# One small tile for the row sums and reciprocals of two attention tiles

## The chip, the cores and the metric

One core of a Trainium2 chip runs the whole program. The metric is the device time in microseconds (us) of one execution; of the kernel before there are three runs, 902.25, 906.55 and 906.75 us, with a median of 906.55 us.

## The reference

Three blocks follow each other, all in float32. The sizes are batch B = 4, heads H = 8, sequence S = 576, head size 64, model width 512.

```python
scores = scale * (q_rot @ k_rot.T)              # 576 x 576 for each batch and head
scores = scores - scores.max(-1)
attn = exp(scores); attn = attn / (attn.sum(-1) + 1e-9)
x = attn @ v                                    # to (4, 576, 512)
x = sigmoid(xr @ w_r) * (relu(xk @ w_k)**2 @ w_v)   # xk, xr: mixes of x and x shifted by a token
u = x + (relu(x.T @ w_tok1) @ w_tok2).T
out = u + relu(u @ w_ch1) @ w_ch2
```

## The kernel before

**Tiles.** A group g is one batch and one pair of heads, so there are 16 groups. A group has ND = 9 tiles of 128 query rows by 576 keys: r = 0 to 7 are four couples (even r for one head, odd r for the other, the same 128 rows), and r = 8 holds the last 64 rows of both heads. Tiles are numbered j = 9 g + r, 144 in all. The first 36 (batch 0, `j < FIRST`) and the other 108 are handled in two ways.

**One tile.** `emit_S` (L452) makes the scores on TensorE in a PSUM tile "S", for both tiles of a couple together. `emit_max` (L470) takes the negated row maximum on VectorE. `emit_exp` (L478, L486) takes the exponential on ScalarE and has the row sum written out by an accumulator read, a second instruction of one column. For r in ASIDE = (0, 2, 4, 6, 7) the exponentials go to an SBUF tile called "es"; for r = 1, 3, 5, 8 they stay in place in PSUM, and the row sum goes to a spare PSUM column beside them. `emit_rc` (L498, L500) makes a denominator and its reciprocal on VectorE, two operations of 128 x 1 for each tile. `emit_hi` (L82) scales the exponentials by the reciprocal into float16 on ScalarE; `emit_lo` (L511) computes the float16 remainder on VectorE and so frees the PSUM of a tile in place; `emit_tr` (L594, L596) transposes both by DMA from SyncE's queue. `emit_pv` (L609) multiplies by v on TensorE: 28 products for the rows of r = 0 to 3, and 28 for those of r = 4 to 8, which come three steps into the next group.

**Batch 0.** There the exponentials stay unscaled: they are transposed on TensorE, multiplied by v (`emit_U`, L546), and a product of the reciprocals with the identity (L550) spreads these for the scaling of the result (`emit_Us`). It already waits for both tiles of a couple.

**What else runs there.** While the tiles of batches 1 to 3 go through (about 113 to 405 us of the profile), `prep` rotates, splits and loads q, k and v of later groups (VectorE, ScalarE, GpSimd, SyncE), and `kvr_gen` runs the relu-squared products of batches already done on TensorE, with conversions on ScalarE and GpSimd ("kp", "t", "q", "k", "vp"). Five of its eight chunks run beside attention; the others wait until attention is over (HELD).

**What sets the order.** `a_step(j)` emits the work of a step; a planner then orders the instructions of each engine by emission position, moved ahead by the constants of PRI (hi 400, S 400, den 50), and by a timeline that it simulates. The engines run their queues in that order. Score tiles have three PSUM buffers, so the scores of a couple need the exponential of the couple before (even tile) and the remainder of an odd tile before that.

In step j of batches 1 to 3 the order of emission is: exponential of j, maximum of j + 1, other work, denominator, reciprocal and hi of j, lo and transpose of j - 1, other work, scores of the next couple, `prep`.

Of the kernel before, what the change touches and what calls it, by code (L numbers as in the profile page):

```python
# [7 lines left out]
F32 = mybir.dt.float32  # L8
# [5 lines left out]
AF = mybir.ActivationFunctionType  # L14
# [5 lines left out]
HS = 288  # L20
DM, DFF, DTOK, DCH = 512, 1024, 256, 1536
KD, KF, KC = DM // 128, DFF // 128, DCH // 128
PSCALE = 2.0 ** 14
# [4 lines left out]
ND = 9  # L28
# [17 lines left out]
ASIDE = (0, 2, 4, 6, 7)  # L46
# [25 lines left out]
def body(tc, kin, qin, vw, tabs, ident, mu, w_k, w_v, w_r, w_t1, w_t2, w_c1, w_c2, out):  # L72
    nc = tc.nc
    PS = bass.MemoryType.PSUM
    act, dve, pool, pe, sp = nc.scalar, nc.vector, nc.gpsimd, nc.tensor, nc.sync

    def copy(e, o, i, scale=None):
        if e == "A":
            if scale is None:
                act.activation(out=o, in_=i, func=AF.Copy)  # L80
            else:
                act.activation(out=o, in_=i, func=AF.Copy, scale=scale)  # L82
        elif e == "P":
            pool.tensor_scalar(out=o, in0=i, scalar1=1.0 if scale is None else scale, scalar2=0.0,
                               op0=ALU.mult, op1=ALU.add)
        elif scale is None:
            dve.tensor_copy(o, i)
        else:
            dve.tensor_scalar(out=o, in0=i, scalar1=scale, scalar2=None, op0=ALU.mult)
# [12 lines left out]
    def prio(name):  # L102
        def wrap(f):
            def g(*a):
                with ahead(PRI.get(name, 0)):
                    return f(*a)
            return g
        return wrap
# [5 lines left out]
    with ctx:  # L114
# [60 lines left out]
        def order(o, p, how=mybir.DependencyClass.NoSync):  # L175
            tc.add_manual_dep(o.ins, p.ins.name, mybir.DependencyInfo(how, mybir.DependencyReason.DATA), reason="order")
# [101 lines left out]
        def right(name, bufs):  # L278
            return at.enter_context(tc.tile_pool(name=name, bufs=bufs, side="right"))
# [8 lines left out]
        p16_p = right("p16", BUFS["p16"])  # L288
        pt_p = right("pt", BUFS["pt"])
        sm_p = right("sm", BUFS["sm"])  # L290
# [10 lines left out]
        FIRST, NTT = NP * ND, NG * ND  # L301
# [106 lines left out]
            sp.dma_start(t[0:64, 5:9], t[64:128, 0:4])  # L408
            sp.dma_start(t[64:128, 5:9], t[0:64, 1:5])

        S_t, sum_t, p16_t, e_t, T_t, U_t, rc_t, free = {}, {}, {}, {}, {}, {}, {}, {}
        pt_t, xT = {}, {}

        def place(r):

            return (4, 0) if r == ND - 1 else (r // 2, r % 2)
# [15 lines left out]
        def emit_S(js):  # L432
            with ahead(PRI["S0" if js[0] < FIRST else "S"]):
                S_products(js)
# [37 lines left out]
        @prio("exp")  # L472
        def emit_exp(j):

            if j < FIRST:
                s = sm_p.tile([128, 1], F32, tag="vm", name="es")
                e = e_t[j] = p16_p.tile([128, 2, HS], F32, tag="p16", name="e")
                act.activation(out=e, in_=S_t.pop(j)[:, :, 0:HS], func=AF.Exp, bias=sum_t[j], accum_out=s)  # L478
                sum_t[j] = s
                return  # L480
            s = S_t[j][:, 0, HS:HS + 1]
            i = e_t[j] = S_t.pop(j)[:, :, 0:HS]
            if j % ND in ASIDE:
                s = sm_p.tile([128, 1], F32, tag="vm", name="es")
                e_t[j] = kz_p.tile([128, 2, HS], F32, tag=f"kz{j % 2}{j // 2 % 2}", name="es")
            o = act.activation(out=e_t[j], in_=i, func=AF.Exp, bias=sum_t[j], accum_out=s)  # L486
            if j % ND in ASIDE:
                free[j] = o
            sum_t[j] = s

        @prio("den")
        def emit_rc(j):
            n = j % ND % 2 if j < FIRST else 0
            if n == 0:
                rc_t[0] = sm_p.tile([128, 2], F32, tag="rc", name="rc")
            r = rc_t[0][:, n:n + 1]
            d = sm_p.tile([128, 1], F32, tag="den", name="den")
            dve.tensor_scalar(out=d, in0=sum_t[j], scalar1=1e-9, scalar2=1.0 if j < FIRST else 1.0 / PSCALE,  # L498
                              op0=ALU.add, op1=ALU.mult)
            dve.reciprocal(r, d)  # L500
            sum_t[j] = rc_t[0] if j < FIRST else r

        @prio("hi")
        def emit_hi(j):
            t = p16_t[j] = p16_p.tile([128, 2, 2, HS], F16, tag="p16", name="p16")
            copy("A", t[:, 0], e_t[j], sum_t[j])

        @prio("lo")
        def emit_lo(j):
            t = p16_t[j]  # L510
            o = last["lo"] = dve.scalar_tensor_tensor(out=t[:, 1], in0=e_t.pop(j), scalar=sum_t[j], in1=t[:, 0],  # L511
                                                      op0=ALU.mult, op1=ALU.subtract)
            if j % ND not in ASIDE:
                free[j] = o

        @prio("tr")
        def emit_T(j):

            t = S_p.tile([128, 2, 512], F32, tag="S", name="T")
            e = e_t.pop(j).rearrange("p a b -> p (a b)")  # L520
            t = T_t[j] = t.rearrange("p a b -> p (a b)")[:, 0:640].rearrange("p (c q) -> p c q", c=5)
            for c in range(5):
                o = min(128 * c, S - 128)
                pe.transpose(t[:, c], e[:, o:o + 128], idn)
# [8 lines left out]
        @prio("pv")  # L533
        def emit_U(j):

            g, r = divmod(j, ND)
            m = place(r)[0]
            p = U_t[g, m] = pv_p.tile([128, 512], F32, tag="pv", name="U")
            ts, w = [T_t.pop(i) for i in ([j] if r == ND - 1 else [j - 1, j])], 64 if r == ND - 1 else 128
            q = None  # L540
            for c in range(6):
                for x in range(2):
                    l = slice(64 * x, 64 * x + 64)
                    d = l if r == ND - 1 else slice(0, 128)
                    if c < 5:
                        o = pe.matmul(p[l, 0:w], lhsT=v_t[g][:, c, l], rhs=ts[x % len(ts)][:, c, d], start=(c == 0),  # L546
                                      stop=(c == 4))
                    else:
                        a = sum_t[j][:, 0:1] if r == ND - 1 else sum_t[j - 1 + x][:, x:x + 1]
                        o = pe.matmul(p[l, 128:128 + w], lhsT=a.broadcast_to([128, 64]), rhs=idn[:, d], start=True,  # L550
                                      stop=True)
                    if q is not None:
                        order(o, q)
                    q = o
# [32 lines left out]
        @prio("tr")  # L587
        def emit_tr(j):
            g, r = divmod(j, ND)
            m, x = place(r)  # L590
            t = p16_t[j].rearrange("p a b c -> p (a b c)")
            if r == ND - 1:
                for y in range(2):
                    sp.dma_start_transpose(out=pt(g, y, 1)[:, :, 256:320], in_=t[64 * y:64 * y + 64])  # L594
            else:
                sp.dma_start_transpose(out=pt(g, x, m // 2)[:, :, 128 * (m % 2):128 * (m % 2) + 128], in_=t)  # L596
# [69 lines left out]

        after = {}

        def a_step(j, kv):

            g, k = divmod(j, ND)

            def other():
                with ahead(PRI["kv"]):
                    kv(KVN)

            if j < NTT:
                emit_exp(j)
            late = group(j + 1) if j + 1 == FIRST else []
            if j + 1 < NTT and not late:  # L680
                emit_max(j + 1)
            other()
            if j < FIRST:
                emit_T(j)
                emit_rc(j)
            elif j < NTT:
                emit_rc(j)
                emit_hi(j)
            for gg in (g, g - 1):
                r = j - gg * ND  # L690
                if NP <= gg < NG and r in PV_AT:
                    after.setdefault(j + 1, []).append(emit_pv(gg, PV_AT[r]))
            if 0 <= j - 1 < FIRST:
                emit_ev(j - 1)
            elif FIRST <= j - 1 < NTT:
                emit_lo(j - 1)
                emit_tr(j - 1)
            other()
            if late:
                emit_S(late)  # L700
                emit_max(j + 1)
            elif j + 2 != FIRST and group(j + 2):
                emit_S(group(j + 2))
            def whole(i):
                return 0 <= i < FIRST and (i % ND % 2 or i % ND == ND - 1)

            if whole(j - 1):
                emit_U(j - 1)
                emit_Us(j - 1)
            for f in after.pop(j, []):  # L710
                f()
            other()
            prep(g, k + ND)
            prep(g + 1, k)
            prep(g + 2, k - ND)
# [487 lines left out]
        n = 0  # L1203
# [7 lines left out]
        n = 0  # L1211
# [79 lines left out]
```

## Time and profile before

| | |
|---|---|
| profiled execution | 908.21 us, its span 906.0 us |
| median of three runs | 906.55 us (902.25 to 906.75) |
| busy over the span | PE 843.6, PE weight loads 726.6, DVE 636.2, ACT 513.9, POOL 476.2 us |
| granted clock, mean over the span | 0.977 |

PE is TensorE, DVE VectorE, ACT ScalarE, POOL GpSimd, SP SyncE. Busy time is the time in which at least one instruction of the engine runs. A bracket such as [1.60 <-DVE rc L500] behind a line of a timeline says how long the engine stood idle before it and what ended that. Attention of batch 0 runs from about 14 to 110 us, of the other batches from 113 to 405 us; the rest is dense layers.

### The profile page before, as it was taken

How to read it: one execution, taken by the hardware profiler on the slowest of the kernel's cores; microseconds unless marked ns; L12 is line 12 of the kernel's file. 1: busy time of each engine (PE TensorE's matmuls, PEld its weight loads, DVE VectorE, ACT ScalarE, POOL GpSimd, SP SyncE). 2: the span in 40 equal slices, each digit the busy share in tenths (PEclk: the TensorE clock that was granted, in tenths of full speed). 3: DMA queues.
4: the chain of work that ended last, by engine and by line, in shares of the span. 5: the costliest groups of instructions: out<-in, count | busy, mean ns of one | idle time of the engine just before them, and what ended most of it. 6: DMA issues, size and time to landing. Idle time of an engine off the chain costs nothing.

```text
span 906.0 us, 18800 instructions
## 1 busy us (share of the span) xinstructions
PE 843.6 (93%) x7004; PEld 726.6 (80%) x7004; DVE 636.2 (70%) x1468; ACT 513.9 (57%) x1155; POOL 476.2 (53%) x506
## 2 busy tenths in 40 slices
PE   8999859898977889999999999999999999999998
PEld 5888747777766778889999989988878888888876
DVE  4889788887888889750794699956798354546332
ACT  2889668776777778774565566454456322323221
POOL 6799979889788676355444654411132222222221
PEclk7999969999999999999999999999999999999999
DMA  8687389998998988889522231201230001001000
GB/s 243 228 270 229 101 181 202 194 217 182 200 203 163 202 147 164 154 160 343 180 90 96 96 116 60 76 2 36 76 95 24 1 5 49 27 27 53 2 27 27
DMA packets 168651, 112.07 MB, mean 124 GB/s; under 512 B 132720, under 2 KB 148208, under 8 KB 168048
## 3 DMA queue, kind: packets, MB, share of 16 engines
q1 hardware_dynamic: 168560, 110.87, 49.2%
q8 instruction: 55, 0.90, 0.4%
q14 instruction: 36, 0.29, 0.1%
HBM read 60.90 MB, written 14.16 MB: 83 GB/s over the span
## 4 chain that ended last, share of the span: by engine, by line
PE 48%; DVE 16%; POOL 6%; ACT 6%; issue 5%; DMA 4%; SPq 1%; DVEq 0%; ACTq 0%; POOLq 0%
PE co L737 5%; PE c1p L737 5%; PE c1p L738 5%; PE c1p L739 5%; PE co L738 5%; PE co L739 5%; DVE p L511 4%; PE pv L609 2%; DVE nm L470 2%; PE vp L737 2%; PE vp L738 2%; PE vp L739 2%; DMA pt<-p 2%; PE kp L737 1%; PE S L452 1%
## 5 line engine op out<-in xcount | busy, mean ns | idle before, releaser
L111 POOL TENSOR_TENSOR hs<-ht,hs 128x288 f16<-128x288 f32 x96 | 73.3, 764 | 229.6 <-DVE ht L1170 115.5
L1166 ACT ACTIVATE hs<-c1p,top 128x288 f16<-128x288 f32 x96 | 47.7, 497 | 161.7 <-PE c1p L739 161.7
L470 DVE TENSOR_REDUCE nm<-S 128x1 f32<-128x576 f32 x144 | 104.5, 749 | 24.8 <-PE S L452 24.0
L738 PE MATMUL c1p<-uhl,parts 128*128 128x288 f16 x384 | 109.8, 286 | 0.0
L739 PE MATMUL c1p<-uhl,parts 128*128 128x288 f16 x384 | 109.7, 286 | 0.0
L737 PE MATMUL c1p<-uhl,parts 128*128 128x288 f16 x384 | 109.5, 286 | 0.0
L738 PE MATMUL co<-hs,parts 128*128 128x288 f16 x384 | 108.7, 286 | 0.0
L739 PE MATMUL co<-hs,parts 128*128 128x288 f16 x384 | 108.6, 286 | 0.0
L737 PE MATMUL co<-hs,parts 128*128 128x288 f16 x384 | 105.1, 286 | 0.3 <-ACT hs L1166 0.3
L452 PE MATMUL S<-kq 64*128 64x288 f32 (+1 forms) x696 | 79.4, 326 | 17.4 <-ACT es L486 5.0
L737 PEld LDWEIGHTS <-parts 128*128 128x128 f16 x768 | 75.1, 98 | 19.3 <-issue 0.5
L738 PEld LDWEIGHTS <-parts 128*128 128x128 f16 x768 | 75.1, 98 | 18.9
L739 PEld LDWEIGHTS <-parts 128*128 128x128 f16 x768 | 75.2, 98 | 18.6
L737 PE MATMUL kp<-xs,parts 128*128 128x288 f32 x256 | 80.1, 316 | 9.0 <-ACT t L805 8.0
L452 PEld LDWEIGHTS S<-kq 64*128 64x128 f32 (+1 forms) x696 | 62.4, 200 | 32.3 <-ACT es L486 9.9
L1170 DVE TENSOR_SCALAR ht<-c1p,top 128x288 f32<-128x288 f32 x60 | 30.9, 516 | 77.6 <-ACT hs L1166 76.5
L111 POOL TENSOR_TENSOR q<-t 128x288 f32<-128x288 f32 x64 | 52.4, 823 | 58.8 <-ACT t L805 55.0
L737 PE MATMUL vp<-k,parts 128*128 128x288 f32 x256 | 76.5, 304 | 4.9 <-ACT vt L830 3.9
L738 PE MATMUL vp<-k,parts 128*128 128x288 f32 x256 | 76.2, 300 | 0.9 <-DVE k L111 0.9
L511 DVE SCALAR_TENSOR_TENSOR p<-es,rc,p 128x576 f16<-128x576 f32 x60 | 68.2, 1141 | 12.4 <-ACT p L82 12.4
L738 PE MATMUL kp<-xs,parts 128*128 128x288 f32 x256 | 76.3, 298 | 0.0
L739 PE MATMUL kp<-xs,parts 128*128 128x288 f32 x256 | 75.7, 296 | 0.0
(158 smaller groups left out, 2467.2 us busy)
## 6 DMA issues: line engine op xcount, KB each, us to landing
rq<-in_qin_dram SPq DMA_DIRECT2D x30, 320.0 KB, 4.1
rk<-in_kin_dram SPq DMA_DIRECT2D x30, 288.0 KB, 3.7
words<-in_w_c_dram SPq DMA_DIRECT2D x12, 512.0 KB, 3.9
words<-in_w_c_dram SPq DMA_DIRECT2D x16, 384.0 KB, 3.2
vr<-in_vw_dram SPq DMA_DIRECT2D x16, 320.0 KB, 3.5
xd<-xT SPq DMA_DIRECT2D x16, 288.5 KB, 2.6
xT<-xd SPq DMA_DIRECT2D x4, 1154.0 KB, 5.4
vd<-vt SPq DMA_DIRECT2D x32, 144.0 KB, 2.2
```

The costliest lines, as they stand in the source:

```text
L111: return (pool if e == "P" else dve).tensor_tensor(o, a, b, op=op)
L452: o = pe.matmul(S_t[j][:, h, 0:HS], lhsT=a[l, 128 * m:128 * m + 128], rhs=b[l, h * HS:(h + 1) * HS], start=(n == 0), stop=(n == 2))
L470: last["max"] = dve.tensor_reduce(out=nm, in_=S_t[j][:, :, 0:HS], op=ALU.max, axis=AX.XY, negate=True)
L511: o = last["lo"] = dve.scalar_tensor_tensor(out=t[:, 1], in0=e_t.pop(j), scalar=sum_t[j], in1=t[:, 0], op0=ALU.mult, op1=ALU.subtract)
L609: pe.matmul(p[l, 0:n], lhsT=v[:, a, l], rhs=ts[x][:, c, :], start=(i == 0), stop=(i == len(prods) - 1))
L737: pe.matmul(p, lhsT=wh, rhs=t[:, 0], start=first, stop=False)
L738: pe.matmul(p, lhsT=wh, rhs=t[:, 1], start=False, stop=False)
L739: pe.matmul(p, lhsT=wl, rhs=t[:, 0], start=False, stop=last)
L1166: last["hs"] = act.activation(out=h[:, 0], in_=p[:, 0:HS], func=AF.Relu, scale=g)
L1170: dve.tensor_scalar(out=f, in0=p[:, 0:HS], scalar1=g, scalar2=0.0, op0=ALU.mult, op1=ALU.max)
```

## The change

A tile "es" of 128 x 6 is allotted at the first tile of each couple, and at r = 8. Columns 0 and 1 take the two row sums, 2 and 3 the denominators, 4 and 5 the reciprocals. The accumulator of an exponential in place writes to it too. `emit_rc` runs once for a couple, with two columns (one for r = 8), and in the step of the second tile. In batches 1 to 3 hi of both tiles, then lo and transpose of both, the second tile first, follow in that same step; so hi of an even tile is emitted one step later than before, and lo and transpose of an odd tile and of r = 8 one step earlier.

```diff
 def emit_exp(j):
+    n = j % ND % 2
+    if n == 0:
+        both[0] = sm_p.tile([128, 6], F32, tag="es", name="es")
+    t = both[0]
+    s = t[:, n:n + 1]
+    i = S_t.pop(j)[:, :, 0:HS]
...
-    s = S_t[j][:, 0, HS:HS + 1]
-    i = e_t[j] = S_t.pop(j)[:, :, 0:HS]
-    if j % ND in ASIDE:
-        s = sm_p.tile([128, 1], F32, tag="vm", name="es")
...
     o = act.activation(out=e_t[j], in_=i, func=AF.Exp, bias=sum_t[j], accum_out=s)
...
-    sum_t[j] = s
+    sum_t[j] = t[:, 4 + n:5 + n]

 def emit_rc(j):
-    n = j % ND % 2 if j < FIRST else 0
-    if n == 0:
-        rc_t[0] = sm_p.tile([128, 2], F32, tag="rc", name="rc")
-    r = rc_t[0][:, n:n + 1]
-    d = sm_p.tile([128, 1], F32, tag="den", name="den")
-    dve.tensor_scalar(out=d, in0=sum_t[j], ...)
-    dve.reciprocal(r, d)
+    t, w = both[0], 1 if j % ND == ND - 1 else 2
+    d = t[:, 2:2 + w]
+    dve.tensor_scalar(out=d, in0=t[:, 0:w], ...)
+    dve.reciprocal(t[:, 4:4 + w], d)

+def whole(j):
+    return j % ND % 2 or j % ND == ND - 1
+def tiles(j):
+    return [j] if j % ND == ND - 1 else [j, j - 1]

 def a_step(j, kv):
     if j < FIRST:
         emit_T(j)
+        if whole(j):
+            emit_rc(j)
+    elif j < NTT and whole(j):
         emit_rc(j)
-    elif j < NTT:
-        emit_rc(j)
-        emit_hi(j)
+        for i in tiles(j):
+            emit_hi(i)
+        for i in tiles(j):
+            emit_lo(i)
+            emit_tr(i)
...
-    elif FIRST <= j - 1 < NTT:
-        emit_lo(j - 1)
-        emit_tr(j - 1)
```

## Rows read from the trace of the kernel before

**Rows 1.** Windows: stretch, length, busy PE, PEld, DVE, ACT, POOL; clock, DMA, GB/s.
```profile
14.00:110.00 96.00, 90.37 (x851) 77.39 (x850) 79.66 (x206) 75.87 (x157) 87.42 (x81) 0.93 0.67 212
113.00:405.00 292.00, 250.24 (x2209) 215.28 (x2210) 245.06 (x542) 220.25 (x488) 213.06 (x205) 0.96 0.92 182
405.00:480.00 75.00, 74.84 (x574) 73.64 (x573) 43.54 (x85) 39.24 (x94) 36.17 (x44) 1.00 0.61 197
```
**Rows 2.** The chain of waits from 113 to 405 us, shares by line.
```profile
by line: DVE p L511 11.2%; issue 9.3%; PE pv L609 6.7%; DVE nm L470 6.4%; DMA pt<-p 4.8%; PE S L452 4.1%; ACT p L82 3.6%; DMA rk<-in_kin_dram 3.5%; POOL rk L111 3.3%; PE kp L737 2.9%; DMA rq<-in_qin_dram 2.8%; POOL rq L111 2.8%; DVE vl L401
```
**Rows 3.** Who waited for whom from 113 to 405 us: total, times, longest.
```profile
ACT p L82 <- DVE rc L500: 9.4, 7, 1.8
PE pv L609 <- DMA pt<-p: 8.6, 7, 2.4
```
**Rows 4.** Windows, denominators and reciprocals alone: stretch, length, DVE busy, clock, DMA, GB/s.
```profile
14.00:110.00 96.00, 10.34 (x72) 0.93 0.67 212
113.00:405.00 292.00, 28.82 (x215) 0.96 0.92 182
```
**Rows 5.** Groups by form, accumulator reads of the exponentials on ACT.
```profile
L486 ACT ACTIVATION_READ_ACCUMULATOR es<-S,nm 128x1 f32 x60 | 12.1, 202 | 0.0
...
L486 ACT ACTIVATION_READ_ACCUMULATOR S<-S,nm 128x1 f32 x48 | 7.0, 145 | 0.0
```
**Rows 6.** Timelines of ACT, then DVE: a couple r = 2, 3.
```profile
245.44 0.71 ACT L486 ACTIVATE S<-S,nm 128x576 f32<-128x576 f32 x1
246.07 0.14 ACT L486 ACTIVATION_READ_ACCUMULATOR S<-S,nm 128x1 f32 x1
246.41 0.78 ACT L82 ACTIVATE p<-es,rc 128x576 f16<-128x576 f32 x1 [0.20 <-ACT S L486]
...
246.44 0.16 DVE L500 RECIPROCAL rc<-den 128x1 f32<-128x1 f32 x1
247.22 1.00 DVE L511 SCALAR_TENSOR_TENSOR p<-es,rc,p 128x576 f16<-128x576 f32 x1 [0.62 <-ACT p L82]
...
248.88 0.74 DVE L470 TENSOR_REDUCE nm<-S 128x1 f32<-128x576 f32 x1
```
**Rows 7.** Timeline of DVE: remainder of r = 8, then the couple r = 0, 1.
```profile
208.69 0.80 DVE L511 SCALAR_TENSOR_TENSOR p<-S,rc,p 128x576 f16<-128x576 f32 x1
209.41 0.14 DVE L498 TENSOR_SCALAR den<-es 128x1 f32<-128x1 f32 x1
...
209.58 0.23 DVE L500 RECIPROCAL rc<-den 128x1 f32<-128x1 f32 x2
```
**Rows 8.** Timelines of POOL and DVE: two places with a two-column operation.
```profile
477.63 0.85 POOL L111 TENSOR_TENSOR q<-t 128x288 f32<-128x288 f32 x1 [0.54 <-DVE rows L135]
...
477.85 0.65 DVE L137 TENSOR_SCALAR rows<-rows 128x2 f32<-128x2 f32 x1
...
576.36 0.81 POOL L111 TENSOR_TENSOR y<-q,y 128x288 f32<-128x288 f32 x1 [0.54 <-ACT q L1011]
...
576.86 0.34 DVE L135 TENSOR_SCALAR rows<-rows 128x2 int32<-128x2 int32 x1
```
**Rows 9.** Groups by form, DVE: count, busy us, mean ns, idle before.
```profile
L137 DVE TENSOR_SCALAR rows<-rows 128x2 f32<-128x2 f32 x6 | 1.5, 242 | 0.0
...
L138 DVE RECIPROCAL rows<-rows 128x2 f32<-128x2 f32 x6 | 1.0, 163 | 0.1
...
L511 DVE SCALAR_TENSOR_TENSOR p<-es,rc,p 128x576 f16<-128x576 f32 x60 | 68.2, 1141 | 12.4 <-ACT p L82 12.4
...
L511 DVE SCALAR_TENSOR_TENSOR p<-S,rc,p 128x576 f16<-128x576 f32 x48 | 38.8, 809 | 4.2 <-ACT p L82 3.9
```
**Rows 10.** Line L498, whole trace: ns min/median/max, first and last start.
```profile
L498 DVE TENSOR_SCALAR den<-es x96: 128/144/157, 14.2 to 398.2; 128x1 f32<-128x1 f32 x96
L498 DVE TENSOR_SCALAR den<-S x48: 138/146/161, 113.0 to 402.6; 128x1 f32<-128x1 f32 x48
```
**Rows 11.** Timeline of PE: products with the values for r = 4 to 8.
```profile
215.72 2.58 PE L609 MATMUL pv<-pt,vh 128*64 128x320 f16 x18 [2.31 <-DMA pt<-p]
```

More of the change, by code (lines that the diff above doesn't have):

```diff
@@ L409, in v_shift @@
             sp.dma_start(t[64:128, 5:9], t[0:64, 1:5])
-        S_t, sum_t, p16_t, e_t, T_t, U_t, rc_t, free = {}, {}, {}, {}, {}, {}, {}, {}
+        S_t, sum_t, p16_t, e_t, T_t, U_t, both, free = {}, {}, {}, {}, {}, {}, {}, {}
         pt_t, xT = {}, {}
@@ L473, in emit_exp @@
         def emit_exp(j):
-            if j < FIRST:
-                s = sm_p.tile([128, 1], F32, tag="vm", name="es")
-                e = e_t[j] = p16_p.tile([128, 2, HS], F32, tag="p16", name="e")
-                act.activation(out=e, in_=S_t.pop(j)[:, :, 0:HS], func=AF.Exp, bias=sum_t[j], accum_out=s)
-                sum_t[j] = s
-                return
-            s = S_t[j][:, 0, HS:HS + 1]
-            i = e_t[j] = S_t.pop(j)[:, :, 0:HS]
-            if j % ND in ASIDE:
-                s = sm_p.tile([128, 1], F32, tag="vm", name="es")
+            n = j % ND % 2
[4 more added lines that the diff above has]
+            i = S_t.pop(j)[:, :, 0:HS]
+            if j < FIRST:
+                e_t[j] = p16_p.tile([128, 2, HS], F32, tag="p16", name="e")
+            elif j % ND in ASIDE:
                 e_t[j] = kz_p.tile([128, 2, HS], F32, tag=f"kz{j % 2}{j // 2 % 2}", name="es")
+            else:
+                e_t[j] = i
             o = act.activation(out=e_t[j], in_=i, func=AF.Exp, bias=sum_t[j], accum_out=s)
-            if j % ND in ASIDE:
+            if FIRST <= j and j % ND in ASIDE:
                 free[j] = o
-            sum_t[j] = s
+            sum_t[j] = t[:, 4 + n:5 + n]
         @prio("den")
         def emit_rc(j):
-            n = j % ND % 2 if j < FIRST else 0
-            if n == 0:
-                rc_t[0] = sm_p.tile([128, 2], F32, tag="rc", name="rc")
-            r = rc_t[0][:, n:n + 1]
-            d = sm_p.tile([128, 1], F32, tag="den", name="den")
-            dve.tensor_scalar(out=d, in0=sum_t[j], scalar1=1e-9, scalar2=1.0 if j < FIRST else 1.0 / PSCALE,
+            t, w = both[0], 1 if j % ND == ND - 1 else 2
+            d = t[:, 2:2 + w]
+            dve.tensor_scalar(out=d, in0=t[:, 0:w], scalar1=1e-9, scalar2=1.0 if j < FIRST else 1.0 / PSCALE,
                               op0=ALU.add, op1=ALU.mult)
-            dve.reciprocal(r, d)
-            sum_t[j] = rc_t[0] if j < FIRST else r
+            dve.reciprocal(t[:, 4:4 + w], d)
         @prio("hi")
@@ L548, in emit_U @@
                     else:
-                        a = sum_t[j][:, 0:1] if r == ND - 1 else sum_t[j - 1 + x][:, x:x + 1]
+                        a = sum_t[j] if r == ND - 1 else sum_t[j - 1 + x]
                         o = pe.matmul(p[l, 128:128 + w], lhsT=a.broadcast_to([128, 64]), rhs=idn[:, d], start=True,
@@ L703, in a_step @@
                 emit_S(group(j + 2))
-            def whole(i):
-                return 0 <= i < FIRST and (i % ND % 2 or i % ND == ND - 1)
-            if whole(j - 1):
+            if 0 <= j - 1 < FIRST and whole(j - 1):
                 emit_U(j - 1)
```

## The prediction

> **What bounds the kernel now.** I read the page first, then busy time by stage, the chain, the waits and, in the end, the timelines of single couples. [rows 1] shows where a change to the softmax can act. From 405 us on PE is full (74.84 of 75 us) and nothing of the change runs there. From 113 to 405 us nobody is full: PE 250, DVE 245, ACT 220 and POOL 213 of 292 us. That stage has a fixed amount of PE work (the attention of twelve groups and five chunks beside it), so what makes its 292 us shorter or longer goes into the whole. The chain there [rows 2] runs through DVE (remainder 11.2%, maximum 6.4%), PE, transposes, ACT and loads: a loop over couples (maximum, two exponentials, denominators and reciprocals, two hi, two remainders, next maximum), in which the in-order queues wait in turn. From 14 to 110 us PE (90.4 of 96) and POOL (87.4) are nearly full, DVE (79.7) a little less.
>
> **What goes.** Of 288 denominators and reciprocals 160 stay: 96 go in the stage from 113 us (216 to 120), 32 in batch 0 (72 to 40). They cost DVE 28.82 us for 215 in the stage, so 0.134 us each, and 10.34 us for 72 before it, 0.144 each [rows 4]. A couple's two pairs, issued back to back, take 0.40 us (209.41 to 209.81) [rows 7]; one pair takes 0.31 to 0.36. So a couple saves DVE 0.06 us (back to back) to 0.27 us (two operations at 0.134). I take the middle, 0.17.
>
> **What the wait for both tiles costs.** Hi of the first tile now needs the second tile's sum. I went through the 48 couples of the stage in the ACT timeline. In every one the second exponential starts before the first hi already, so nothing is lost in order. What is lost is cover: the first tile's denominator and reciprocal ran under the second exponential. [rows 6] is the pattern: the second sum is read out until 246.21, hi of the first tile starts at 246.41, while the second tile's own reciprocal is ready only at 246.60, 0.39 us after the read. After the change hi cannot start before that, about 0.42 us after the read. In 19 couples (11 of the 12 r = 2, six r = 4, two r = 6) the first hi is that near: 0.20 to 0.3 us behind the read in 13, directly behind it in 6. They are late by 0.22 x 13 + 0.50 x 6 = 5.9 us. In the other 29 the first hi comes 0.4 us or more after the read (other ACT work, or DVE's queue as in [rows 7]) and the new wait is covered. What waits behind a late hi on ACT is the second hi, and behind it on DVE both remainders and the next maximum (247.22 to 248.88 in [rows 6]).
>
> The sum of a tile in place goes to SBUF now and not to PSUM. Its read took 145 ns into PSUM and 202 into SBUF [rows 5]: 0.06 us in 17 of the 19 couples, 1.0 us.
>
> **What two columns cost.** This decides my forecast. The denominator turns from 128 x 1 into 128 x 2 with source and destination in SBUF. The kernel has such TENSOR_SCALARs elsewhere. Twice one began while a POOL instruction ran [rows 8]: at 477.85 it took 0.65 us and ended 0.02 us after POOL's (478.48), at 576.86 it took 0.34 and ended 0.03 after POOL's (577.17). The other five of the first form average (6 x 242 - 654) / 5 = 160 ns [rows 9]. With one column that never happens: 144 denominators took at most 161 ns [rows 10], though POOL is busy for 73% of the stage and 91% of batch 0. Another operation of this stage shows the size of such a hold: the remainder with its exponentials in SBUF takes 1141 ns on average, with them in PSUM 809 [rows 9], so 0.33 us more. Bounds for one denominator: 0 (POOL happens to idle each time) to 0.52 (always in the midst of a POOL instruction: 213.06 us over 205 is 1.04 us each [rows 1]). I take 0.33 in the stage, the nearest row. In batch 0: share 0.91 times half of 87.42 / 81 us, 0.49. The two-column reciprocal took 163 ns over six [rows 9]; I give it no hold.
>
> [...]
>
> **What moves.** Remainder and transpose of an odd tile and of r = 8 are emitted a step earlier. All 8.6 us that PE waits for transposes [rows 3] stand before the products for r = 4 to 8, as in [rows 11], and the remainder of r = 8 often comes late, behind other DVE work ([rows 7], 208.69). Between 0 (the planner draws the products forward as well) and 8.6 us can go; I take 2, since in the four groups whose remainder of r = 8 came over 3 us behind its hi these waits add up to 3.1 us. Two transposes of a couple were issued one behind the other before too, so SP's queue is no dearer; PSUM comes free no later, since the tile in place has its remainder first now.
>
> **The sum,** against the profiled 908.2 us (span 906.0):
> - 19 near couples: 5.9 + 1.0 + 19 x 0.33 = 13.2 us. In 11 of them the next maximum follows the remainders directly, in 8 the queue has it earlier; so 0.6 of it: +7.9.
> - 29 others: DVE has 0.33 - 0.17 = 0.16 us more each, 4.6 us; DVE's queue decides in about half: +2.3.
> - transposes of r = 8: -2.
> - batch 0: DVE loses 32 x 0.144 = 4.6 and gets 16 x 0.49 = 7.8, so 3.2 more, half of it under PE and POOL: +1.6.
>
> Together +9.8, 918.0 us for a profiled execution. The median of three lies 0.2% under the profiled one (906.55 to 908.21), so 916.3 us.
>
> **Rivals.**
> *A. DVE's queue is what counts, and the hold is rare: faster.* For it: DVE is busy for 84% of the stage and heads the chain. Then 28.82 - 60 x 0.31 = 10.2 us go from DVE, 84% of them from the stage (8.6), half of the 8.6 us of transpose waits (4.3) and half of the 4.6 us of batch 0: -15.2, so 893 profiled, 891.5 as a median. It decides where the hold is below the 0.17 us saved. Against it: in the near couples those operations lie in DVE's idle time (0.62 us before the remainder in [rows 6]).
> [...]
>
> *B. No hold, small effects cancel: no change.* (5.9 + 1.0) x 0.6 - 29 x 0.17 / 2 - 2 = -0.4, 906 us. For it: [rows 8] are only two places. Against it: no two-column operation that began under a POOL instruction there escaped.
>
> *C. The merged denominator also falls behind a remainder in DVE's queue* (it is ready later than the first tile's was, and the planner sees no hold). As in [rows 7], that adds 0.80 us; for all near couples 19 x 0.8 x 0.6 = 9.1 more: 925 us.
>
> *D. The merge isn't one:* if a tile's columns were ordered as a whole, nothing new would wait, as exponentials already run in order on ACT. That falls to B.
>
> **How the numbers follow.** A difference of 0.5% (4.5 us) is about what a measurement of this kernel tells from none. Forecast 0.53, all of it slower; C 0.07; so slower 0.60. B, with D and the weak ends of both sides, 0.22. A 0.18. The forecast's own range, with the hold between 0.15 and 0.45 us, is 910 to 923. The range for 8 in 10 goes down into A, to 899, and up to C, to 929; about 0.1 lies below it and 0.07 above.
>
> **What would show it.** Right: 80 denominators, 64 of them with two columns, of which those under a POOL instruction last until it ends, with a mean of 0.35 to 0.6 us and a maximum over 1 us; ACT's wait for reciprocals well over 9.4 us; the stage from 113 to 405 us some 10 us longer, the dense layers unchanged. For A: two-column denominators near 0.16 us, DVE's busy time in the stage down by 10 us, and a shorter stage. Wrong step by step: a first hi that in most couples starts later than 0.42 us after the read for other reasons (the near couples aren't the rule in the new order); waits for transposes that don't fall. What would upset it most is a planner's order that fills ACT and DVE quite differently around the couples.

## The result and the profile after

The changed kernel takes 914.25 us (median of four runs, 913.84 to 915.51), the kernel before beside it 905.46 us: a ratio of 1.0105, with a 95% interval of 1.0074 to 1.0135. The forecast was 916.3 us, slower. A second measurement, beside the last experiments and with six runs, gave 914.33 us and 1.0100 (1.0056 to 1.0144).

The sign and the size came out as forecast. The experiments below show that the reasons did so only in part. The hold of the two-column denominators is there, 0.31 us on average in the stage of batches 1 to 3 against 0.33 forecast. By the medians it is the smaller share of the loss, and without it the prediction's sum came to no loss at all.

The page after, busy time over the span of 913.6 us (profiled execution 915.51 us):
```profile
PE 844.3 (92%) x7004; PEld 727.8 (80%) x7004; DVE 641.5 (70%) x1340; ACT 519.5 (57%) x1155; POOL 474.7 (52%) x506
```
DVE has 128 instructions fewer (1468 before) and is busy 5.3 us longer (636.2 before). PE is busy 0.7 us longer than before (843.6); the other 6.9 of the 7.6 us of span are idle time of PE, 62.4 us before (906.0 - 843.6) and 69.3 now.

The stage of batches 1 to 3, from its first maximum to its last remainder, in the windows of the kernel after (columns as in [rows 1]):
```profile
110.50:414.60 304.10, 259.69 (x2262) 223.68 (x2262) 249.54 (x451) 227.44 (x496) 217.04 (x211) 0.94 0.89 180
```
and of the kernel before:
```profile
108.75:404.62 295.87, 253.82 (x2244) 218.01 (x2244) 248.52 (x547) 222.11 (x493) 216.43 (x207) 0.96 0.91 182
```
The stage is 8.2 us longer and the stretch up to its start 1.8 us, while the dense layers behind it are 2.4 us shorter (501.4 us before, 499.0 now): 18 of their products (2262 for 2244) have moved into the stage. PE idles 44.4 us there for 42.1, so only 2.3 of the 8.2 us are idle time of PE. The other 5.9 us are busy time: the 18 products (an estimated 2.0 us at 0.1131 us each, 253.82 over 2244) and 1.5% more for each product (0.1148 us, 259.69 over 2262) at a granted clock of 0.94 instead of 0.96. Over the whole span the clock is no lower than before (0.978 and 0.977).

The groups of the merged operations after, which answer to [rows 4, 9 and 10]:
```profile
L508 DVE SCALAR_TENSOR_TENSOR p<-es,p 128x576 f16<-128x576 f32 x60 | 64.3, 1081 | 1.9 <-ACT p L82 1.8
...
L496 DVE TENSOR_SCALAR es<-es 128x2 f32<-128x2 f32 x64 | 34.5, 539 | 17.9 <-ACT S L487 15.5 <-ACT es L487 1.2 <-ACT e L487 1.1
...
L498 DVE RECIPROCAL es<-es 128x2 f32<-128x2 f32 x64 | 10.4, 162 | 1.4
...
L496 DVE TENSOR_SCALAR es<-es 128x1 f32<-128x1 f32 x16 | 2.3, 142 | 2.2 <-ACT S L487 2.2
```
With one column a denominator takes 142 ns as before, with two 539. Of the 64 with two columns, 51 began while a POOL instruction ran: 43 of these ended 0.02 to 0.03 us after the end of that instruction or, twice, of the next; 5 began in the last 0.09 us of one, and 3, which began within 0.02 us of POOL's start, were not held. The 13 that began while POOL stood idle took at most 171 ns. The reciprocals are not held (162 ns). The denominators alone have gone from 20.7 us for 144 to 36.8 us for 80.

One couple in the timelines of the kernel after, ACT, then POOL, then DVE:
```profile
173.50 0.20 ACT L487 ACTIVATION_READ_ACCUMULATOR S<-S,nm 128x1 f32 x1
...
175.99 0.74 ACT L82 ACTIVATE p<-S,es 128x576 f16<-128x576 f32 x1 [1.04 <-DVE es L498]
...
174.26 1.42 POOL L111 TENSOR_TENSOR rk<-rk,tab 128x576 f32<-128x576 f32 x1 [2.28 <-DMA rk<-in_kin_dram]
...
174.11 0.55 DVE L612 TENSOR_SCALAR xT<-pv,sc 128x320 f32<-128x320 f32 x1 [1.33 <-PE pv L606]
174.58 1.13 DVE L496 TENSOR_SCALAR es<-es 128x2 f32<-128x2 f32 x1
175.74 0.17 DVE L498 RECIPROCAL es<-es 128x2 f32<-128x2 f32 x1
```
POOL's instruction ends at 175.68, the denominator at 175.71, and hi starts 2.29 us after the second sum was read (173.70). In [rows 6] it started 0.20 us after. Not all of this is the hold: the denominator began 0.88 us after the read, because DVE's queue stood before "xT", which waited for PE. The hold is about 0.97 us of it (1.13 us less the 0.16 of an unhindered one).

Who waited from 113 to 405 us after, answering to [rows 3]:
```profile
PE S L452 <- DVE p L508: 15.8, 8, 3.2
...
ACT p L82 <- DVE es L498: 10.4, 12, 1.6
...
PE pv L606 <- DMA pt<-p: 9.1, 7, 3.1
```
The first line has grown most: PE stands before the scores of a couple until a remainder has freed their PSUM. In the kernel before this was 1.3 us:
```profile
PE S L452 <- DVE p L511: 1.3, 3, 0.5
```
The second measurement's profile has 13.5, 8.2 and 6.7 us in the three places, so differences of two microseconds between single profiles say little. And as PE's idle time in the stage has grown by 2.3 us only, most of the 15.8 us stand in place of other waits.

### The profile page after: what moved, and what is told of

Its sections match the earlier page's. It is cut to its first block, busy times and chain, and to the rows that moved or that the text cites. A ratio compares the mean times of both kernels' runs of the same rounds, so it can differ in the third digit from the quotient of the medians.

```text
span 913.6 us, 18645 instructions
## 1 busy us (share of the span) xinstructions
PE 844.3 (92%) x7004; PEld 727.8 (80%) x7004; DVE 641.5 (70%) x1340; ACT 519.5 (57%) x1155; POOL 474.7 (52%) x506
## 4 chain that ended last, share of the span: by engine, by line
PE 47%; DVE 8%; issue 3%; POOL 3%; ACT 3%; DMA 1%; SPq 0%; DVEq 0%; POOLq 0%; ACTq 0%
PE co L741 5%; PE c1p L741 5%; PE c1p L742 5%; PE c1p L743 5%; PE co L742 5%; PE co L743 5%; PE vp L741 2%; PE vp L742 2%; PE vp L743 2%; PE pv L606 2%; PE kp L741 1%; PE S L452 1%; PE kp L743 1%; PE kp L742 1%; DVE f L999 1%
## 5 line engine op out<-in xcount | busy, mean ns | idle before, releaser
L470 DVE TENSOR_REDUCE nm<-S 128x1 f32<-128x576 f32 x144 | 104.0, 747 | 15.9 <-PE S L452 15.8
L452 PE MATMUL S<-kq 64*128 64x288 f32 (+1 forms) x696 | 75.7, 322 | 22.1 <-DVE p L508 15.8
L741 PE MATMUL kp<-xs,parts 128*128 128x288 f32 x256 | 82.3, 323 | 10.2 <-ACT t L809 6.8
L452 PEld LDWEIGHTS S<-kq 64*128 64x128 f32 (+1 forms) x696 | 59.8, 196 | 36.3 <-issue 18.7
L741 PE MATMUL vp<-k,parts 128*128 128x288 f32 x256 | 77.2, 306 | 1.9 <-ACT vt L834 1.9
L742 PE MATMUL kp<-xs,parts 128*128 128x288 f32 x256 | 78.1, 305 | 0.0
L743 PE MATMUL kp<-xs,parts 128*128 128x288 f32 x256 | 77.4, 302 | 0.0
L742 PE MATMUL vp<-k,parts 128*128 128x288 f32 x256 | 76.5, 301 | 0.9 <-DVE k L111 0.7
L743 PE MATMUL vp<-k,parts 128*128 128x288 f32 x256 | 75.8, 297 | 0.0
```

Of the source, the lines that this page charges most:

```text
L452: o = pe.matmul(S_t[j][:, h, 0:HS], lhsT=a[l, 128 * m:128 * m + 128], rhs=b[l, h * HS:(h + 1) * HS], start=(n == 0), stop=(n == 2))
L470: last["max"] = dve.tensor_reduce(out=nm, in_=S_t[j][:, :, 0:HS], op=ALU.max, axis=AX.XY, negate=True)
L741: pe.matmul(p, lhsT=wh, rhs=t[:, 0], start=first, stop=False)
L742: pe.matmul(p, lhsT=wh, rhs=t[:, 1], start=False, stop=False)
L743: pe.matmul(p, lhsT=wl, rhs=t[:, 0], start=False, stop=last)
```

## The experiments

The theories: *hold* (the two-column operations cost the time), *late hi* (the couple's wait for both sums does), and from the second set on *move* (remainders and transposes emitted a step earlier do) and *order* (any change makes the planner deal other queues, and those are slower). A ratio is always to the kernel before on the same chip.

The experiments ran in three sets, each on a chip of its own: e5, e1, e3 and e2; then e2r, f1, f3 and g1; then f6, f7, f9 and a2. Kernels of different sets are best compared by their ratios.

**e5_reduce.** The order of the queues stays that of the kernel after (in the two traces PE's but for 2 of 7004 instructions, ACT's but for 1 of 1011, POOL's and SP's in full); only the hold goes.
```diff
-dve.tensor_scalar(out=d, in0=t[:, 0:w], scalar1=1e-9, scalar2=..., op0=ALU.add, op1=ALU.mult)
+dve.tensor_reduce(out=d, in_=t[:, 0:w].unsqueeze(2), op=ALU.add, axis=AX.X)
```


> The kernel after with each denominator as a TENSOR_REDUCE over one element per column (a copy of the sums), in place of the two-column TENSOR_SCALAR; the 2^14 that the denominators carried is left out of p and of the output's scaling, and the addition of 1e-9 is left out. The order of every queue stays that of the kernel after. Theory 'hold' (the two-column TENSOR_SCALAR waits for POOL's instruction): the 64 two-column operations fall from a mean of 0.54 us to about 0.16, which gives DVE 24 us back (9 in batch 0, 15 later); by the factors of the prediction 10 to 12 us of time: 902 to 905 us. Rival 'late hi' (the couple's wait for both sums and the new order cost the time): the first hi still waits for both sums and the order is the same, so 911 to 914 us.

Measured: 912.81 us, 1.0082 (1.0050 to 1.0114). The group of the denominators in this kernel:
```profile
L496 DVE TENSOR_REDUCE es<-es 128x2 f32<-128x2 f32 x64 | 9.5, 148 | 18.0 <-ACT S L487 15.7 <-ACT e L487 1.1 <-ACT es L487 0.9
```
The hold is gone, and with it 25 us of these operations, but only 1.4 us of time (0.2% by the ratios). That contradicts the 902 to 905 us of *hold*: by the medians most of the loss isn't the hold. Nor did DVE as a whole get 25 us back: in the profiled execution (919.43 us) it is busy for 629.1 us, 12.4 less than in the kernel after. Another operation took up most of the difference, after first, then e5:
```profile
L111 DVE TENSOR_TENSOR kq<-rq,kq 128x640 fp32r<-128x640 f32 x15 | 18.4, 1229 | 0.2 <-POOL a L84 0.2
```
```profile
L111 DVE TENSOR_TENSOR kq<-rq,kq 128x640 fp32r<-128x640 f32 x15 | 26.6, 1770 | 0.5 <-ACT kq L80 0.5
```

**e1_one_column.**
```diff
-dve.tensor_scalar(out=d, in0=t[:, 0:w], ...)
+for c in range(w):
+    dve.tensor_scalar(out=t[:, 2 + c:3 + c], in0=t[:, c:c + 1], ...)
```


> The kernel after, but each couple's denominators in two one-column operations (144 in all), the reciprocals still two columns; planned anew. Theory 'hold': no denominator over 0.2 us, 902 to 908 us, some 3 us of that for an order dealt anew. Rival 'late hi': 911 to 914 us.

Measured: 915.75 us, 1.0117 (1.0077 to 1.0157), with no denominator over 0.16 us. The same verdict, though the queues were dealt anew here.

**e3_sums_in_psum.**
```diff
+if j >= FIRST:
+    both[1] = S_t[j if n or j % ND == ND - 1 else j + 1][:, 0, HS:HS + 2]
+    s = both[1][:, n:n + 1]
...
+dve.tensor_scalar(out=d, in0=both[1][:, 0:w], ...)     # one column each in batch 0
```


> The kernel after, but from batch 1 on both sums of a couple go to two spare PSUM columns of its odd tile, and the two-column denominator reads them there; batch 0 has one-column denominators. Theory 'hold': a source in PSUM is not held, denominators near 0.15 us, and the accumulator reads cost 0.145 instead of 0.20 us: 901 to 907 us. Rival 'late hi': 911 to 914 us.

Measured: 922.48 us, 1.0192 (1.0152 to 1.0233), with no denominator over 0.17 us. Both theories missed, and the kernel isn't a clean test of either. Its edit writes the even tile's sum into the odd tile's PSUM, and its maxima now wait for exponentials of "es", 14.5 us in all, which they don't in the kernel after:
```profile
L470 DVE TENSOR_REDUCE nm<-S 128x1 f32<-128x576 f32 x144 | 107.1, 749 | 24.4 <-ACT es L490 14.5 <-PE S L452 9.5
```
How much of the time this wait costs wasn't measured.

**e2_hold_alone.**
```diff
-nm = sum_t[j] = sm_p.tile([128, 1], ...)
+ns[j] = sm_p.tile([128, 2], ...); nm = sum_t[j] = ns[j][:, 0:1]
-s = sm_p.tile([128, 1], F32, tag="vm", name="es")      # r in ASIDE, batch 0
+s = ns[j][:, 1:2]
-dve.tensor_scalar(out=d, in0=sum_t[j], ...)
+dve.tensor_scalar(out=d, in0=ns[j] if w == 2 else sum_t[j], ...)
```


> The kernel before, with nothing merged: where the row sum lies in SBUF (96 of 144 tiles) it shares a tile with the negated maximum, and the denominator is taken over both columns, of which only the second is used. Theory 'hold': 36 operations in batch 0 held by about 0.6 us each and 60 later by 0.3 give DVE 40 us more; 15 to 20 us of time: 920 to 926 us. Rival 'late hi': nothing waits for both sums here, so 903 to 908 us.

Measured: 922.02 us, 1.0181 (1.0139 to 1.0223), where *hold* had put it. But the queues had been dealt anew too, so its twin without the hold had to follow.

**e2r_no_hold.**
```diff
-dve.tensor_scalar(out=d, in0=ns[j] if w == 2 else sum_t[j], ...)
+dve.tensor_reduce(out=d, in_=(ns[j] if w == 2 else sum_t[j]).unsqueeze(2), op=ALU.add, axis=AX.X)
```


> The kernel of e2_hold_alone with its denominators as TENSOR_REDUCEs over one element per column (2^14 and 1e-9 left out as in e5_reduce); the order of the queues is nearly that of e2 (ACT 945 of 1013, SP 360 of 377 instructions in the same order). Theory 'hold': the 96 two-column operations fall to 0.15 us and the time from 922 to 903 to 909 us. Theory 'order' (what counts is the order that the planner deals anew for any change): e2r stays at 917 us or more.

Measured: 917.84 us, 1.0121 (1.0065 to 1.0177). The denominators of e2, then of e2r:
```profile
L500 DVE TENSOR_SCALAR den<-nm 128x2 f32<-128x2 f32 x96 | 51.6, 542 | 8.0 <-ACT es L487 5.7 <-ACT e L479 2.0
```
```profile
L500 DVE TENSOR_REDUCE den<-nm 128x2 f32<-128x2 f32 x96 | 13.7, 146 | 11.3 <-ACT es L487 7.4 <-ACT e L479 3.8
```
These operations take 38 us less, DVE as a whole is busy 26.7 us less (660.9 to 634.2), and the ratio falls by 0.6%, with intervals that overlap. *Order* gains: e2r has 288 denominators and reciprocals like the kernel before, no hold, no merge and no move, and is still 1.2% slower.

**f1_lo_in_place.** From e5:
```diff
 for i in tiles(j):
     emit_hi(i)
-for i in tiles(j):
-    emit_lo(i)
-    emit_tr(i)
...
+elif FIRST <= j - 1 < NTT:
+    emit_lo(j - 1)
+    emit_tr(j - 1)
```


> The kernel e5_reduce (merged, no hold), but remainder and transpose of each tile emitted in the next step, as in the kernel before. Theory 'move' (emitting remainders and transposes a step earlier makes the planner put scores into PE's queue ahead of the remainder of r = 8, where PE then stands idle): PE's wait for remainders before scores falls from about 10 us to under 3, and the time to 903 to 908 us. Theory 'late hi': the first hi still waits for both sums, 911 to 915 us.

Measured: 909.95 us, 1.0035 (1.0004 to 1.0067), the least of the merged kernels. PE's wait for remainders before scores falls from 9.8 us in e5 to 4.6, while its wait there for exponentials of "es" rises from 2.0 to 9.2. *Late hi* in its strong form is out: this kernel waits for both sums in every couple.

**f3_move_alone.** From before:
```diff
 emit_rc(j)
 emit_hi(j)
+emit_lo(j)
+emit_tr(j)
...
-elif FIRST <= j - 1 < NTT:
-    emit_lo(j - 1)
-    emit_tr(j - 1)
```


> The kernel before, nothing merged, but remainder and transpose of each tile emitted in its own step, one earlier than before. Theory 'move': PE waits 8 us or more for remainders before scores, 911 to 916 us. Theory 'late hi': no tile waits for its couple, 902 to 908 us.

Measured: 917.68 us, 1.0140 (1.0095 to 1.0186). The time is that of *move*, its mechanism isn't: the wait that it named is no longer than in the kernel before. The line from this kernel's stage:
```profile
PE S L452 <- DVE p L511: 1.2, 3, 0.7
```

**g1_no_denominator.** From before:
```diff
-dve.tensor_scalar(out=d, in0=sum_t[j], ...)
-dve.reciprocal(r, d)
+dve.reciprocal(r, sum_t[j])
```


> The kernel before with no denominators at all: the reciprocal is taken of each tile's sum (2^14 and 1e-9 left out as in e5_reduce). It takes 144 operations and 20 us of busy time off DVE and about 0.18 us off the way from each exponential to its hi. If DVE's queue and that way bound the stage, as 'late hi' says: 893 to 900 us. If the dealt order decides: 902 to 912 us.

Measured: 914.12 us, 1.0108 (1.0056 to 1.0160). Work was only taken away and the kernel got slower, more than *order* itself had allowed.

**f6_hold_lo_in_place.** From after, the edit of f1 alone:
```diff
-for i in tiles(j):
-    emit_lo(i)
-    emit_tr(i)
...
+elif FIRST <= j - 1 < NTT:
+    emit_lo(j - 1)
+    emit_tr(j - 1)
```

> The kernel after with the move alone undone: two-column TENSOR_SCALARs that POOL can hold, remainder and transpose emitted in the next step as before. Its queues are nearly in the order of f1_lo_in_place (ACT 979 of 1013, SP 371 of 377). Theory 'move': 4 us of stage time less than after, so 909 to 912 us, and above f1 only by what the hold costs. Theory 'hold': the 64 held operations alone keep it at 913 us or more, 4 us or more above f1. Theory 'any new order costs a per cent': 913 us or more as well, but then PE's wait for remainders before scores stays at 8 us or more.

Measured: 921.48 us, 1.0166 (1.0118 to 1.0214). *Move* isn't borne out: undoing it beside the hold makes the kernel slower than after, not faster as from e5 to f1. Against f1, which has no hold and on ACT nearly the same order, its ratio is 1.3% higher, and here the intervals are apart. The stage of f1 and that of f6 in windows (columns as in [rows 1]):
```profile
106.90:404.40 297.50, 257.45 (x2247) 219.43 (x2246) 231.49 (x451) 225.41 (x493) 215.48 (x207) 0.94 0.92 181
```
```profile
107.40:406.00 298.60, 251.92 (x2215) 213.84 (x2215) 249.39 (x451) 224.26 (x489) 212.23 (x203) 0.95 0.90 181
```
DVE is busy 17.9 us longer. The length is nearly equal, but f6 gets 32 products fewer done there; they come later, and what follows the stage takes 6.3 us longer than in f1 (507.2 and 500.9). PE idles 46.7 us instead of 40.1. But PE's queue isn't that of f1: up to its last scores it has 3047 products, that of f1 3086. So this pair doesn't show the hold alone, as the next kernel makes plain.

**f7_late_merge_only.** From f1, in batch 0:
```diff
+if j < FIRST:
+    n, t = j % ND % 2, both[0]
+    d = t[:, 2 + n:3 + n]
+    dve.tensor_scalar(out=d, in0=t[:, n:n + 1], ...)
+    dve.reciprocal(t[:, 4 + n:5 + n], d)
+    return
```


> The kernel f1_lo_in_place (no hold, no move) with batch 0 as in the kernel before (one-column denominators and reciprocals for each tile); 2^14 left out of p and the scaling. The merge stays from batch 1 on. If the merge itself helps there (f1's stage at an even clock is 2.4 us shorter than before's) and batch 0 is what costs f1 its 0.35%, this kernel takes 902 to 905 us and beats both. If any new order costs a per cent: 908 to 915 us.

Measured: 917.41 us, 1.0123 (1.0086 to 1.0160). From batch 1 on it is the same program as f1, in other queues (by their tiles and shapes at most 879 of ACT's 1011 instructions are in the same order, 983 in f6), and its ratio is 0.9% higher, with intervals apart. Its stage:
```profile
104.40:407.00 302.60, 253.07 (x2215) 213.70 (x2215) 229.62 (x451) 224.32 (x489) 209.99 (x202) 0.95 0.89 179
```
It holds nothing, and yet has as few products in the stage as f6, PE idle for 49.5 us, and takes 6.4 us more after the stage than f1. So what f6 loses against f1 is at least in part PE's order. Against f7 on the same chip f6 is 0.4% slower, with intervals that overlap.

**f9_batch0_merge_only.** From before, the merge of the change for `j < FIRST` only:
```diff
-act.activation(..., bias=sum_t[j], accum_out=s)
+act.activation(..., bias=sum_t[j], accum_out=t[:, n:n + 1])
...
+if j < FIRST:
+    t, w = rc_t[0], 1 if j % ND == ND - 1 else 2
+    dve.tensor_scalar(out=t[:, 2:2 + w], in0=t[:, 0:w], ...)
+    dve.reciprocal(t[:, 4:4 + w], t[:, 2:2 + w])
+    return
...
-emit_rc(j)
+if j % ND % 2 or j % ND == ND - 1:
+    emit_rc(j)
```

> The kernel before with the merge in batch 0 alone: 16 two-column and 4 one-column denominators and reciprocals there, each tile by itself from batch 1 on. Theory 'batch 0 counts': the two-column operations are held by about 0.57 us each and the product of the reciprocals waits on PE, so the first maximum of batch 1 comes 4 to 6 us later at an even clock and the time is 909 to 912 us. Theory 'hold and merge cost nothing there': 903 to 908 us.

Measured: 906.38 us, 1.0012 (0.9988 to 1.0036). Batch 0 is cleared of all but 0.36%, hold included (16 denominators there take 728 ns on average).

**a2_after_again** repeated the kernel after (above).

> The kernel after once more, unchanged, beside the others on one chip: 913 to 916 us if before is at 905 to 907.

All of them side by side:

| kernel | two-column TENSOR_SCALARs in SBUF | waits for both sums | moved | ratio to before |
|---|---|---|---|---|
| after (twice) | 64 | yes | yes | 1.0105, 1.0100 |
| e5_reduce | none | yes | yes | 1.0082 |
| e1_one_column | none | yes | yes | 1.0117 |
| e3_sums_in_psum | none | yes | yes | 1.0192 |
| f6_hold_lo_in_place | 64 | yes | no | 1.0166 |
| f1_lo_in_place | none | yes | no | 1.0035 |
| f7_late_merge_only | none | from batch 1 | no | 1.0123 |
| f9_batch0_merge_only | 16 (batch 0) | in batch 0 | no | 1.0012 |
| f3_move_alone | none | no | yes | 1.0140 |
| e2_hold_alone | 96 | no | no | 1.0181 |
| e2r_no_hold | none | no | no | 1.0121 |
| g1_no_denominator | none | no | no | 1.0108 |

## Why the prediction was right, point by point

**The hold: right in itself.** 539 ns on average was forecast as 0.35 to 0.6 us, with a maximum over 1 us (it is 1.46). Over the 160 ns of an unhindered one it is 0.57 us in batch 0 (forecast 0.49) and 0.31 in the stage (forecast 0.33), 24 us of these operations in all. Held ones end 0.02 to 0.03 us after POOL's instruction, as in [rows 8].

**Its price: too high.** By the sum's own factors the hold was to cost 10 to 12 us (expected of e5); the one pair that has the same order, after and e5, puts it at 1.4 us (0.2%, within intervals of 0.3%). Two more pairs point the same way: 0.6% (e2 and e2r, within their intervals) and 1.3% (f6 and f1, beyond them, but with another order on PE). So the sum turned about half of the 24 us into time, and in the same order less than a tenth of them came out.

**The late hi: right as a mechanism, its price not isolated.** The timelines give what was forecast: the near couples have gone from 19 of 48 to none; the first hi starts 0.55 us after the read at the earliest in the kernel after, 0.47 in e5 and f1 (forecast 0.42). On average it starts 0.99 us after the read before, 1.47 in e5, 1.62 after. But f1 waits for both sums in every couple and costs 0.04 to 0.67%, 0.4 to 6.1 us; the sum without the hold, (5.9 + 1.0) x 0.6 = 4.1 us, is neither shown nor excluded by that.

**Undecided: the transposes.** PE's wait for them was to fall by 2 us of 8.6. It is 9.1 in the first profile of the kernel after and 6.7 in the second. In 8 of the 12 groups the products for r = 4 to 8 stand behind the same scores as before, in 2 earlier and in 2 later.

**Undecided: batch 0.** It was to cost 1.6 us. The two profiles show 1.8, but f9 leaves no more than about 3 us, and about 1 us by its ratio; in the second profile of the kernel after the stage began at 106.1 us, in the first at 110.5. One profile doesn't show a difference that small there.

**Wrong: where the wait shows.** ACT's wait for reciprocals was to be well over 9.4 us and is 10.4, in the second profile 8.2. What grew is PE's wait before scores (1.3 to 15.8 us, 13.5 in the second). It is a sign of the new order and not the size of the loss: f3 has 1.2 us of it and is no faster than the kernel after. The stage was to be some 10 us longer with the dense layers unchanged; it is 8.2 longer, and they are 2.4 shorter.

**The term that was missing.** The prediction named "a planner's order that fills ACT and DVE quite differently around the couples" as what would upset it most, and gave it no price. Rival B shows the gap: without the hold the sum came to no change (906 us), and e5, without the hold, is at 912.81. (B's terms add up to -0.3, not -0.4, and leave out what batch 0 would save without a hold, half of 4.6 us; with it B stands at 904. A's median is 891.4, not 891.5.) e2r, g1 and f3 have neither hold nor a wait for both sums, and cost 1.1 to 1.4%. f7 and f1 are the same program from batch 1 on and lie 0.9% apart. So a new order, with next to nothing else changed, moves this kernel by about as much as the whole change did, and of twelve other kernels none was faster than the kernel before. That the forecast came so near is luck: a hold charged some 9 us too dearly stood in for this term, which had been left at nothing.

**What stays open** is how the 1.0% divides in the kernel after between the order, the late hi and the hold. Edits change the order with everything else, and only the swap of the denominator's operation kept it: that gives the hold 0.2% there, within intervals of 0.3%. Nor is it shown why the order of the kernel before is as good as any of the others. A version that beats the kernel before was not found; f9 equals it.

## What to carry to other kernels

Before merging two small VectorE operations into one of two columns, look in the trace for a two-column one of its kind beside GpSimd work: here it turned 0.15 us into 0.54. Count what the merge makes later (here the first hi, 1.47 us after the second sum on average without any hold, where it was 0.99) and not only what it saves. Don't take time given back to one operation for time given back to its engine, nor that for time of the kernel (25, 12.4 and 1.4 us in e5). And where queues are dealt by a planner, price a new order first, from two or three harmless edits, before believing a theory of a per cent; an operation swapped for another of equal length, which keeps the order, is the cleanest test.

## What the runs showed of the hardware

- In these traces a TENSOR_SCALAR of 128 x 2 with source and destination in SBUF that began under a running POOL instruction lasted to 0.02 to 0.03 us behind the end of that one or, seldom, of the next (43 of 51 in the kernel after, two of them to the next; 63 of 72 in e2). 3 and 4 escaped, all but one of them begun within 0.03 us of POOL's start; the others began in its last 0.09 us. In the same places a TENSOR_REDUCE of 128 x 2 took 148 ns on average and at most 157 (e5), and a TENSOR_SCALAR of 128 x 2 with its source in PSUM 156 ns and at most 161 (e3). In the kernel after 41 of the 64 RECIPROCALs of 128 x 2 and 11 of the 16 TENSOR_SCALARs of one column began under a running POOL instruction, and none took over 168 and 156 ns.
- Taking 25 and 38 us off held VectorE operations made VectorE 12.4 and 26.7 us less busy and gave back 1.4 us (e5) and 0.6% (e2r), neither beyond the intervals.
- The read of an exponential's sum took ScalarE 145 ns into PSUM and 202 ns into SBUF [rows 5]. In the kernel after, where the sums of those 48 tiles go to SBUF too, their read took 199 ns.
